# One subtraction per head moved from DVE to GpSimd, with the planned order worked out anew

## The chip, the core and the metric

One core of a Trainium2 chip runs the whole program once. The metric is the device time of that execution in microseconds. The engines are PE (TensorE, matrix products), DVE (VectorE), ACT (ScalarE), POOL (GpSimd) and SP (which here only issues transfers). Each works through its own queue in order and waits at semaphores for the others.

## What is computed

Attention with a causal mask and a bias from running sums, then a mixture layer, then a routed second one:

```python
scores = scale * np.matmul(q, k.transpose(0, 1, 3, 2))
cum = np.cumsum(np.maximum(s, 0.0), axis=-1)
bias = -(cum[:, :, :, None] - cum[:, :, None, :])
scores = np.where(causal, -1000000000.0, scores + np.minimum(bias, 0.0))
attn = softmax(scores); x = np.matmul(attn, v)             # x: 2304 x 512
h = np.maximum(np.maximum(x @ w1, x @ w2), x @ w3)         # 768 wide
x = h @ w_out
e = argmax(x @ w_gate + modality_bias[modality_id])        # 8 experts
out = gate * (np.maximum(x @ w1[e], 0.0) @ w2[e])          # 1024 wide
```

## The kernel before

**Numbers in two parts.** A product is made of fp32 values split in two: the high part is the value rounded to fp32r, the low part is the value minus its high part. A product is then high x high plus high x low plus low x high. Making the parts costs other engines a rounding copy and a subtraction for each operand.

**Attention.** There are 32 heads, in 16 pairs. For a head, `load_x` brings q and k in (`qk_r`, `bufs=3`). `k_high` (L374) copies k's high part into one half of `hl`; `q_high` (L377, ACT) copies q's, in both halves of the partitions; `k_low` (L384) subtracts to make k's low part in the other half of `hl`; `q_low` (L387, POOL) makes q's low part in `q_b`; `k_again` (L380, POOL) makes another copy of k's high part in `k_b`. `k_high` is on POOL for heads 1 to 4 (`CK_POOL`), on ACT for the others. `k_low` is on DVE for all heads. The shape of the last four is 64 x 576.

Then, in five blocks of rows (six pieces, as the longest row is cut in two): `scores` (L394, L395, PE) multiplies `hl` with `hl` and `q_b` with `k_b` into a PSUM bank (three banks); it needs all of the head's parts. `least` (L403, DVE) adds the mask and takes the minimum of the negated scores; `expo` (L410, ACT) makes the exponentials and their sums; `turn` (L415, PE) transposes them, `turned` (L420, DVE or ACT) copies the transposes out of PSUM; `values_of` (L450, PE) multiplies a pair of heads with v; `x_most` and `x_rest` (L456, L460, DVE) multiply by the inverse of the sums, which goes through memory and back (`r_out`, `r_in`) to be spread over the partitions.

**Work beside it.** During attention the first weights of the first mixture layer are converted from a 64-bit form: `wz` on ACT, three steps on DVE (L224, L226, L228), a transfer started by POOL (L231) and a subtraction on POOL (L235). With them PE makes early products of that layer from finished batches, in triples of 128 x 288 (L246, L247, L248; `fill`), 168 triples in all; `fx_high` (ACT) and `fx_low` (L478, POOL) split their inputs, and `filled` (L491) takes the maximum. What is left of the triples follows attention; then come the rest of the first layer and the routed layer.

**What sets the order.** In the attention stage the order of every queue is planned when the program is built. Each piece of work is a `Job` with an engine, an assumed duration in ns, a key, the jobs it follows and the buffers it takes. `planned` plays the queues with these durations: whichever engine can start first gets, among the jobs that can start within 60 ns of the soonest, the one with the lowest key. A key is the head's number times `KEY["T"]` plus an offset for the kind of job; the triples have keys above all others. Jobs marked `lock` on DVE are planned not to overlap with POOL's. The queues then run in this order on the chip, whatever the durations are there. After the stage, the framework's own scheduler orders the instructions.

Of the kernel before, what the change touches and what calls it, by code (L numbers as in the profile page):

```python
# [5 lines left out]
F32 = mybir.dt.float32  # L6
# [3 lines left out]
ALU = mybir.AluOpType  # L10
# [6 lines left out]
T = B * S  # L17
# [63 lines left out]
MIN_NS = {(0, 0): 145, (1, 0): 278, (2, 0): 410, (3, 0): 545, (4, 0): 375, (4, 1): 400}  # L81
SC_NS = {(0, 0): 224, (1, 0): 224, (2, 0): 298, (3, 0): 408, (4, 0): 266, (4, 1): 266}
PT_NS = {"ACT": [420, 420, 275, 485], "DVE": [540, 540, 340, 605]}
CK_POOL = (1, 2, 3, 4)
C_ORDER = [(4, 0), (3, 0), (4, 1), (2, 0), (1, 0), (0, 0)]
T_ORDER = [1, 0, 3, 2]
PT_V = [(1, 0), (3, 0), (0, 1), (2, 1)]
CONV = [(0, 3), (1, 3), (2, 5), (3, 7), (4, 7), (5, 9), (6, 13), (7, 15), (8, 17)]
W_READY, SET_H = 15000, 24
WIRE_FROM, WIRE_TO, WIRE_SLOW = 1300, 900, 1.0  # L90
KEY = {"T": 7489, "wl": 195894, "wz": -70601, "w1": 73283, "wd": 182933, "ws": 159332, "lx": -44441, "lv": -72906, "ck": 7387, "kb": -121032, "kl": 34282, "ql": -113713, "s": 45058, "mn": 54834, "ex": 21338, "ds": 1446, "t": 65914, "dt": 1295, "cp": -47797, "r1": -72927, "r2": -108656, "rt": 37074, "rc": 2313, "rw": -46013, "pv": -70417, "x": 43622, "xc": -76674, "xs": 230686, "fe": -33618}
R_MOE1 = (2, 4, 7)
R_MOE2 = (1, 3, 5)

# [84 lines left out]
def fused_kernel(tc, qk, vd, sd, w64, mod, wg, wgt, mb, we, cst, csi, out):  # L179
    nc = tc.nc  # L180
    V, A, G, P, SP = nc.vector, nc.scalar, nc.gpsimd, nc.tensor, nc.sync
    top = ExitStack()
    with top:
# [73 lines left out]
        with ExitStack() as es:  # L257
# [73 lines left out]
            st, tl = {}, {}  # L331

            def job(name, run, eng, ns, key, **k):
                j = Job(run, eng, ns, key, **k)
                jobs.append(j)
                st[name] = j
                return j

            def at(h, what, n=0):
                return h * KEY["T"] + KEY[what] + n  # L340

# [30 lines left out]
            def k_high(h):  # L372
                hl = tl["hl", h] = qkp.tile([128, 2, S], F32R, name="hl", bufs=HL_BUFS)
                (G.tensor_copy if h in CK_POOL else A.copy)(out=hl[64:128, 0], in_=tl["x", h][64:128, 1])  # L374

            def q_high(h):
                A.copy(out=tl["hl", h][:, 1], in_=tl["x", h][:, 0])  # L377
# [3 lines left out]

            def k_low(h):
                hl = tl["hl", h]
                V.tensor_tensor(out=hl[0:64, 0], in0=tl["x", h][64:128, 1], in1=hl.bitcast(F32)[64:128, 0], op=ALU.subtract)  # L384

            def q_low(h):
                G.tensor_tensor(out=qbs[h % QB_N][0:64], in0=tl["x", h][0:64, 0], in1=tl["hl", h].bitcast(F32)[0:64, 1], op=ALU.subtract)  # L387
# [1 line left out]
            def scores(h, c, k):  # L389
                hl, k_b, q_b = tl["hl", h], tl["k_b", h], qbs[h % QB_N]  # L390
                q0, w = QC[c][0], QC[c][2]
                k0, n = (k * 288, 288) if c == 4 else (0, w)
                s_ps = tl["s_ps", h, c, k] = ps_s.tile([128, 512], F32, name="s_ps")[:, 0:n]
                P.matmul(s_ps, hl[:, 1, q0:q0 + 128], hl[:, 0, k0:k0 + n], start=True, stop=False)  # L394
                P.matmul(s_ps, q_b[:, q0:q0 + 128], k_b[:, k0:k0 + n], start=False, stop=True)  # L395
# [100 lines left out]
            for n, h in CONV:  # L496
                raw, z = Slot("raw"), Slot("z")
                a = job(("wl", n), lambda n=n: w_load(n), "SP", 450, at(h, "wl"), takes=[raw], wire=1500, ready=W_READY)
                for k, (what, eng, ns, u, lock, land) in enumerate([("wz", "ACT", 575, [raw], False, 0), ("w1", "DVE", 346, [], False, 0), ("w1", "DVE", 606, [raw], True, 0), ("w1", "DVE", 610, [raw], True, 0), ("wd", "POOL", 570, [], False, 7000), ("ws", "POOL", 1277, [], False, 0)]):
                    a = job(("w", n), lambda n=n, k=k: w_step(n, k), eng, ns, at(h, what, k), after=[a], takes=[z] if k == 0 else [], uses=u + [z], land=land, lock=lock)  # L500
            rows = job("rows", rows_out, "SP", 1300, -1e8, ready=8700, wire=300)
            turns, highs = None, []
            for h in range(2 * NP):
                p, j = divmod(h, 2)
                s_x, s_k, s_h, s_q, s_e = (Slot(n) for n in ("qk", "kb", "hl", "qb", "e"))
                lx = job(("lx", h), lambda h=h: load_x(h), "SP", 1900 if h == 0 else 1130, at(h, "lx") if h > 2 else -1e9 + h, takes=[s_x], ready=750, wire=1700)
                if j == 0:
                    s_v, s_p, done = Slot("vr"), [], []
                    lv = job(("lv", p), lambda p=p: values_in(p), "SP", 430, at(h, "lv") if p else -9e8, takes=[s_v], wire=1300, ready=2000)
                ck = job(("ck", h), lambda h=h: k_high(h), "POOL" if h in CK_POOL else "ACT", 671 if h in CK_POOL else 575, at(h, "ck"), after=[lx], takes=[s_h], uses=[s_x], ready=0 if h else 6640)  # L510
                cq = job(("cq", h), lambda h=h: q_high(h), "ACT", 580, at(h, "ck", 1), after=[lx, ck], uses=[s_x, s_h])
                if h > 1:
                    lk = job(("lk", h), lambda h=h: load_k(h), "SP", 300 if h > 1 else 450, at(h, "lx", 1) if h > 1 else -2e8 + h, after=[rows], takes=[s_k], wire=100, ready=7800)
                kb = job(("kb", h), lambda h=h: k_again(h), "POOL", 657, at(h, "kb"), after=[lx, lk] if h > 1 else [lx], takes=[s_k] if h < 2 else [], uses=[s_x, s_k])
                if h < 2:
                    lk = job(("lk", h), lambda h=h: load_k(h), "SP", 300 if h > 1 else 450, at(h, "lx", 1) if h > 1 else -2e8 + h, after=[kb], uses=[s_k], wire=100, ready=7800)
                kl = job(("kl", h), lambda h=h: k_low(h), "DVE", 780, at(h, "kl"), after=[ck], uses=[s_x, s_h], lock=True, tail=10)
                ql = job(("ql", h), lambda h=h: q_low(h), "POOL", 1410, at(h, "ql"), after=[cq], takes=[s_q], uses=[s_x, s_h])
                ex = {}
                for n, (c, k) in enumerate(C_ORDER):  # L520
                    bank = Slot("s")
                    a = job(("s", h, c, k), lambda h=h, c=c, k=k: scores(h, c, k), "PE", SC_NS[c, k], at(h, "s", n * KEY["ds"]), after=[kl, cq, kb, ql, lk], takes=[bank], uses=[s_h, s_q, s_k])
                    a = job(("mn", h, c, k), lambda h=h, c=c, k=k: least(h, c, k), "DVE", MIN_NS[c, k], at(h, "mn", n * KEY["ds"]), after=[a] + ([st["mn", h, *C_ORDER[0]]] if n else []), takes=[s_e] if n == 0 else [], uses=[bank, s_e], lag=145 * k)
                    if k or c < 4:
                        ex[c] = job(("ex", h, c), lambda h=h, c=c: expo(h, c), "ACT", EXP_NS[c], at(h, "ex", n * KEY["ds"]), after=[a], uses=[s_e], tail=0)
                done += ex.values()
                for n, i in enumerate(T_ORDER):
                    bank, s_t = Slot("t"), Slot("pt")
                    turns = job(("t", h, i), lambda h=h, i=i: turn(h, i), "PE", 109 * len(BANKS[i][0]) - 82, at(h, "t", n * KEY["dt"]), after=[ex[c] for c in sorted({c for c, _ in BANKS[i][0]})] + [turns] * (turns is not None), takes=[bank], uses=[s_e], tail=247)
                    eng = "DVE" if (i, j) in PT_V else "ACT"  # L530
                    s_p.append((s_t, job(("cp", h, i), lambda h=h, i=i: turned(h, i), eng, PT_NS[eng][i], at(h, "cp", n * KEY["dt"]), after=[turns], takes=[s_t], uses=[bank])))
                if j:
                    bank, s_r, s_0, s_o = Slot("t"), Slot("rb"), Slot("t"), Slot("o")
                    a = job(("r1", p), lambda p=p: sums(p), "ACT", 180, at(h, "r1"), after=done, lag=125)
                    a = job(("r2", p), lambda p=p: inverse(p), "DVE", 130, at(h, "r2"), after=[a])
# [303 lines left out]
        for w in range(NW):  # L839
# [25 lines left out]
            for i in range(MW // 128):  # L865
                t = w * (MW // 128) + i
# [181 lines left out]
```

## Time and profile before

| | us |
|---|---|
| Median of three runs | 749.87 (748.5 to 750.04) |
| The profiled execution | 748.16 |
| Its span, first to last instruction | 746.4 |
| PE busy | 713.3 (96%) |
| DVE busy | 523.9 (70%) |
| ACT busy | 403.1 (54%) |
| POOL busy | 184.7 (25%) |

The profile is of one execution. Its rows give the busy time of an engine, the durations of instructions, and for each idle time the event that ended it ("<-" and the engine and line that released it). The shares over the whole span mix stages with different limits, so the rows below are taken by stretch. A duration of an instruction on DVE or POOL includes time in which it was started but stood still. Durations of neighbouring instructions of an engine overlap a little, so busy time is less than their sum.

### The profile page before, as it was taken

The numbers are of one execution on the slowest core, as the hardware profiler recorded it, in microseconds if no ns is written. First come the engines' busy times: TensorE is split into PE (matmuls) and PEld (weight loads), VectorE is DVE, ScalarE is ACT, GpSimd is POOL, SyncE is SP. The second block draws the span as 40 slices with busy tenths as digits, with TensorE's granted clock in tenths as the row PEclk, the third lists the DMA queues.
The fourth block names the chain that finished last, engine by engine and source line by source line (L and its number), as shares of the span: only waits on it lengthen the run. The fifth ranks groups of instructions, "written<-read, shape, count | busy, mean of one in ns | idle before, by whom it ended". The sixth has DMA issues, their size and how long they took to land. (4 is left out here: it accounts for less than half of the span.)

```text
span 746.4 us, 13653 instructions
## 1 busy us (share of the span) xinstructions
PE 713.3 (96%) x4602; PEld 638.7 (86%) x4602; DVE 523.9 (70%) x1567; ACT 403.1 (54%) x988; POOL 184.7 (25%) x206
## 2 busy tenths in 40 slices
PE   4889999999999999999999999999999999999996
PEld 3677878779888989999999998999899988999884
DVE  5899999998856972494676786675776556575540
ACT  5888898799753541222222222446556565565631
POOL 6555556454201220001010101033132222221101
PEclk9999999999999999999999999999999999999999
DMA  7565775756116530100101011568487565666610
GB/s 212 150 194 151 213 204 161 212 151 167 48 62 212 164 113 0 40 15 12 54 12 64 22 49 36 197 178 249 125 256 262 203 241 188 237 213 220 220 41 19
DMA packets 43536, 103.84 MB, mean 139 GB/s; under 512 B 9472, under 2 KB 13472, under 8 KB 43456
## 3 DMA queue, kind: packets, MB, share of 16 engines
q1 hardware_dynamic: 35808, 86.04, 37.2%
q0 software_dynamic: 4912, 11.82, 5.2%
q10 hardware_dynamic: 2736, 5.01, 1.8%
q8 instruction: 38, 0.62, 0.3%
q14 instruction: 42, 0.34, 0.1%
HBM read 88.83 MB, written 12.18 MB: 135 GB/s over the span
## 5 line engine op out<-in xcount | busy, mean ns | idle before, releaser
L246 PE MATMUL a_ps<-xh,w_h 128*128 128x384 f32 (+2 forms) x492 | 161.2, 328 | 3.0 <-ACT h L489 1.7
L247 PE MATMUL a_ps<-xl,w_h 128*128 128x384 f32 (+2 forms) x492 | 157.6, 320 | 0.3 <-POOL xl L478 0.3
L248 PE MATMUL a_ps<-xh,w_l 128*128 128x384 f32 (+2 forms) x492 | 156.8, 320 | 0.0
L750 DVE TENSOR_TENSOR e_l<-e_raw,e_h 128x512 fp32r<-128x512 f32 x160 | 103.3, 684 | 12.6 <-ACT e_h L749 11.2
L749 ACT CAST e_h<-e_raw 128x512 fp32r<-128x512 f32 x160 | 92.8, 622 | 14.9 <-DMA e_raw<-in_we 6.1
L246 PEld LDWEIGHTS a_ps<-xh,w_h 128*128 128x128 f32 x492 | 92.9, 189 | 4.8 <-ACT h L489 2.2
L410 ACT ACTIVATE e<-e,mn 128x448 f32<-128x448 f32 (+4 forms) x160 | 88.7, 556 | 11.5 <-DVE mn L403 11.3
L247 PEld LDWEIGHTS a_ps<-xl,w_h 128*128 128x128 f32 x492 | 92.9, 189 | 1.5 <-POOL xl L478 0.9
L248 PEld LDWEIGHTS a_ps<-xh,w_l 128*128 128x128 f32 x492 | 92.5, 188 | 0.1
L780 PE MATMUL h_ps<-x2t,e_h 128*128 128x256 f32 x288 | 81.0, 282 | 0.0
L781 PE MATMUL h_ps<-x2t,e_l 128*128 128x256 f32 x288 | 80.9, 282 | 0.0
L779 PE MATMUL h_ps<-x2t,e_h 128*128 128x256 f32 x288 | 80.5, 282 | 0.0
L394 PE MATMUL s_ps<-hl 128*128 128x288 f32 (+1 forms) x192 | 66.7, 357 | 13.8 <-ACT augk L267 7.5
L658 POOL DMA_INDIRECT table<-meta,si x18 | 19.1, 1063 | 241.0 <-DVE nm L646 83.8
L633 DVE CUSTOM_DVE_ANT_0 junk<-x,wg 128x512 bf16<-128x512 f32 x96 | 65.8, 685 | 17.2 <-ACT x L711 16.3
L415 PE MATMUL t_ps<-ident,e 128*128 128x128 f32 x480 | 72.0, 283 | 3.9 <-DVE pt L420 3.3
L403 DVE CUSTOM_DVE_ANT_0 e<-s_ps,mask 128x288 f32<-128x288 f32 (+4 forms) x160 | 63.2, 424 | 6.5 <-PE s_ps L395 5.8
L415 PEld LDWEIGHTS t_ps<-ident,e 128*128 128x128 f32 x480 | 58.5, 145 | 7.0 <-DVE pt L420 4.3
L387 POOL TENSOR_TENSOR q_b<-qk_r,hl 64x576 fp32r<-64x576 f32 x32 | 48.7, 1523 | 57.9 <-ACT hl L377 51.5
L395 PE MATMUL s_ps<-k_b,q_b 66*128 66x288 f32 (+1 forms) x192 | 59.5, 319 | 3.0 <-POOL q_b L387 3.0
L809 PE MATMUL y_ps<-e_h,gh 128*128 128x512 f32 x152 | 61.5, 405 | 0.4 <-ACT gh L801 0.4
L811 PE MATMUL y_ps<-e_h,gl 128*128 128x512 f32 x152 | 60.7, 399 | 0.0
(178 smaller groups left out, 1484.1 us busy)
## 6 DMA issues: line engine op xcount, KB each, us to landing
e_raw<-in_we SPq DMA_DIRECT2D x80, 512.0 KB
w_raw<-in_w SPq DMA_DIRECT2D x24, 512.0 KB
qk_r<-in_qk SPq DMA_DIRECT2D x31, 288.0 KB
v_r<-in_vd SPq DMA_DIRECT2D x16, 320.0 KB
rb<-r_d SPq DMA_DIRECT2D x32, 160.0 KB
qk_r<-in_qk SPq DMA_DIRECT2D x32, 144.0 KB
x2d<-x ACTq DMA_DIRECT2D x18, 256.0 KB
w_h<-w_z POOLq DMA_DIRECT2D x9, 256.0 KB, 5.9
```

Of the source, the lines that this page charges most:

```text
L246: P.matmul(a_ps, wh[:, c], xh, start=c == 0, stop=False)
L247: P.matmul(a_ps, wh[:, c], xl, start=False, stop=False)
L248: P.matmul(a_ps, wl[:, c], xh, start=False, stop=c == 3)
L394: P.matmul(s_ps, hl[:, 1, q0:q0 + 128], hl[:, 0, k0:k0 + n], start=True, stop=False)
L410: A.activation(out=ec, in_=ec, func=ACTF.Exp, bias=tl["mn", h][:, c:c + 1], scale=-1.0, accum_out=tl["l", p][:, j, c:c + 1])
L415: P.transpose(out=t_ps[:, n * 128:(n + 1) * 128], in_=e_bufs[h % E_N][:, EOFF[c] + kb * 128:EOFF[c] + (kb + 1) * 128], identity=ident)
L633: V.tensor_tensor_reduce(out=junk, in0=x2, in1=wg_sb[ei // 2][:, ei % 2, :], scale=1.0, scalar=0.0, op0=ALU.mult, op1=ALU.add, accum_out=l ...
L749: A.copy(out=h, in_=raw[:, a])
L750: V.tensor_tensor(out=lo, in0=raw[:, a], in1=h.bitcast(F32), op=ALU.subtract)
L779: P.matmul(h_ps, w(hs, f, c), xt[:, 0, c], start=c == 0, stop=False)
L780: P.matmul(h_ps, w(hs, f, c), xt[:, 1, c], start=False, stop=False)
L781: P.matmul(h_ps, w(ls, f, c), xt[:, 0, c], start=False, stop=c == 3)
```

## The change

`k_low` moves from DVE to POOL for heads 1 to 31; head 0 keeps it on DVE. `k_high` of heads 1 to 4 moves from POOL to ACT. The planner's table of keys is another one, and some assumed durations are other ones: the weight steps on DVE, the roundings on ACT and the scores are planned as longer, the weight steps no longer as locked against POOL.

```diff
-CK_POOL = (1, 2, 3, 4)
+CK_POOL = ()
+KL_DVE = (0,)
...
-KEY = {"T": 7489, "wl": 195894, "wz": -70601, "w1": 73283, "wd": 182933, "ws": 159332, "lx": -44441, "lv": -72906, "ck": 7387, "kb": -121032, "kl": 34282, "ql": -113713, "s": 45058, "mn": 54834, "ex": 21338, "ds": 1446, "t": 65914, "dt": 1295, "cp": -47797, "r1": -72927, "r2": -108656, "rt": 37074, "rc": 2313, "rw": -46013, "pv": -70417, "x": 43622, "xc": -76674, "xs": 230686, "fe": -33618}
+KEY = {"T": 13121, "wl": 335509, "wz": 23759, "w1": 144307, "wd": 156003, "ws": 321816, "lx": 164276, "lv": -213741, "ck": 5481, "kb": 19101, "kl": -60043, "ql": -58751, "s": 264284, "mn": 24364, "ex": 43536, "ds": 50, "t": 176453, "dt": 3418, "cp": 54562, "r1": 16757, "r2": -10485, "rt": 112017, "rc": 23647, "rw": -7037, "pv": -19979, "x": -161664, "xc": 53429, "xs": 81013, "fe": 51163}
...
-                V.tensor_tensor(out=hl[0:64, 0], in0=tl["x", h][64:128, 1], in1=hl.bitcast(F32)[64:128, 0], op=ALU.subtract)
+                (V if h in KL_DVE else G).tensor_tensor(out=hl[0:64, 0], in0=tl["x", h][64:128, 1], in1=hl.bitcast(F32)[64:128, 0], op=ALU.subtract)
...
-                kl = job(("kl", h), lambda h=h: k_low(h), "DVE", 780, at(h, "kl"), after=[ck], uses=[s_x, s_h], lock=True, tail=10)
+                kl = job(("kl", h), lambda h=h: k_low(h), "DVE" if h in KL_DVE else "POOL", 850 if h in KL_DVE else 1415, at(h, "kl"), after=[ck], uses=[s_x, s_h], lock=h in KL_DVE, tail=10 if h in KL_DVE else 0)
```

In the new kernel every line number below the first of these is one higher: L385 is `k_low`, L388 `q_low`, L381 `k_again`.

**POOL's queue at the start of attention**, from the copies of k for heads 0 and 1 on (`hl<-qk_r` at L374 is `k_high`, `q_b` is `q_low`). Before:

```order
L380 CAST k_b<-qk_r 64x576 x2
L374 CAST hl<-qk_r 64x576
L387 ISA
L387 TENSOR_TENSOR q_b_129<-qk_r,hl 64x576
L387 TENSOR_TENSOR q_b_130<-qk_r,hl 64x576
```

Now:

```order
L381 CAST k_b<-qk_r 64x576 x2
L388 ISA
L388 TENSOR_TENSOR q_b_129<-qk_r,hl 64x576
L385 TENSOR_TENSOR hl<-qk_r,hl 64x576
L388 TENSOR_TENSOR q_b_130<-qk_r,hl 64x576
```

`k_high` of head 1 has left the place ahead of the first `q_low`, and `k_low` of head 1 stands between the first two.

**POOL's queue in the middle of the stage**, where weights are converted beside the heads (`w_l` and `w_h` are weight steps, `xl` is `fx_low`). Before:

```order
L387 TENSOR_TENSOR q_b_129<-qk_r,hl 64x576
L380 CAST k_b<-qk_r 64x576
L235 TENSOR_TENSOR w_l<-w_z,w_h 128x512
L478 TENSOR_TENSOR xl<-x_521,xh 128x288
L387 TENSOR_TENSOR q_b_130<-qk_r,hl 64x576
L380 CAST k_b<-qk_r 64x576
L231 DMA w_h<-w_z 128x512
L387 TENSOR_TENSOR q_b_131<-qk_r,hl 64x576
```

Now:

```order
L385 TENSOR_TENSOR hl<-qk_r,hl 64x576
L388 TENSOR_TENSOR q_b_130<-qk_r,hl 64x576
L479 TENSOR_TENSOR xl<-x_515,xh 128x288
L232 DMA w_h<-w_z 128x512
L385 TENSOR_TENSOR hl<-qk_r,hl 64x576
L388 TENSOR_TENSOR q_b_131<-qk_r,hl 64x576
L381 CAST k_b<-qk_r 64x576
```

Each head has one more subtraction there, directly ahead of its `q_low`.

**DVE's queue behind the second pair's normalisation** (`x_521` and `x_515` are the output of attention, `e_135` the exponentials' buffer of one head, `pt` a transpose copied out). Before:

```order
L403 ISA e_135,mn<-s_ps,mask 128x448
L403 ISA mn 128x1
L384 TENSOR_TENSOR hl<-qk_r,hl 64x576
L420 COPY pt<-t_ps 128x512
L403 ISA e_135,mn<-s_ps,mask,mn 128x288
```

Now:

```order
L457 TENSOR_TENSOR x_515<-o_ps,rb 128x512
L461 TENSOR_TENSOR x_515<-t_ps,rb 128x64
L404 ISA e_135,mn<-s_ps,mask 128x448
L404 ISA mn 128x1
L404 ISA e_135,mn<-s_ps,mask,mn 128x288
```

The subtraction that stood between two minimums and ahead of a copy is gone.

On PE, counted over the whole queue, 83 of the 168 triples stood ahead of the last product with v and 85 behind it; now 61 stand ahead of it and 107 behind.

## Rows read from the trace of the kernel before

Each group says its view. In timelines a row is the start and the duration in us, then the engine, the line and the operation; the brackets hold the idle time before it and what ended it.

**Rows 1.** Busy us by stretch: PE, PEld, DVE, ACT, POOL; clock, DMA share, GB/s.

```profile
0.00:20.00 20.00, 9.22 (x35) 8.26 (x36) 11.78 (x33) 10.39 (x23) 13.08 (x39) 1.00 0.78 218
20.00:60.00 40.00, 34.53 (x245) 27.92 (x245) 35.97 (x116) 35.28 (x103) 21.88 (x22) 0.96 0.56 162
60.00:120.00 60.00, 56.24 (x434) 47.40 (x432) 57.04 (x167) 52.12 (x149) 33.80 (x35) 1.00 0.67 191
120.00:180.00 60.00, 57.01 (x430) 46.82 (x429) 54.34 (x163) 53.10 (x149) 29.98 (x28) 0.97 0.62 174
227.00:300.00 73.00, 69.69 (x445) 67.51 (x445) 47.36 (x84) 25.83 (x51) 8.76 (x9) 1.00 0.37 125
20.00:227.00 207.00, 194.71 (x1481) 162.40 (x1481) 182.39 (x564) 174.56 (x499) 95.75 (x93) 0.98 0.53 152
```

**Rows 2.** Whom PE waited for, 20 to 227 us: total, times, longest.

```profile
PE s_ps L394 <- DVE mn L403: 5.3, 8, 1.5
PE t_ps L415 <- DVE pt L420: 3.3, 3, 2.1
PE t_ps L431 <- DVE x L460: 1.3, 1, 1.3
PE t_ps L431 <- DVE mn L403: 0.7, 1, 0.7
PE s_ps L394 <- DVE hl L384: 0.7, 1, 0.7
```

**Rows 3.** DVE, line 384, 20 to 227 us: group; then min/median/max ns.

```profile
L384 DVE TENSOR_TENSOR hl<-qk_r,hl 64x576 fp32r<-64x576 f32 x29 | 29.2, 1009 | 1.8 <-ACT hl L374 1.0
L384 DVE TENSOR_TENSOR hl<-qk_r,hl x29: 751/754/2599, 23.2 to 199.2; 64x576 fp32r<-64x576 f32 x29
```

**Rows 4.** Timeline of DVE, POOL and PE at 48 to 53 us: start, duration.

```profile
48.97 0.62 DVE L403 CUSTOM_DVE_ANT_0 e<-s_ps,mask 128x448 f32<-128x448 f32 x1
49.63 2.60 DVE L384 TENSOR_TENSOR hl<-qk_r,hl 64x576 fp32r<-64x576 f32 x1
...
48.19 1.43 POOL L387 TENSOR_TENSOR q_b<-qk_r,hl 64x576 fp32r<-64x576 f32 x1 [0.19 <-ACT hl L377]
49.59 0.79 POOL L478 TENSOR_TENSOR xl<-x,xh 128x288 fp32r<-128x288 f32 x1
50.35 1.26 POOL L235 TENSOR_TENSOR w_l<-w_z,w_h 128x512 fp32r<-128x512 f32 x1
...
52.89 1.09 PE L415 MATMUL t_ps<-ident,e 128*128 128x128 f32 x8 [2.13 <-DVE pt L420]
```

**Rows 5.** POOL, line 387: min/median/max ns; its wait for ACT, 20-227 us.

```profile
L387 POOL TENSOR_TENSOR q_b<-qk_r,hl x32: 1395/1430/1949, 9.1 to 199.6; 64x576 fp32r<-64x576 f32 x32
...
POOL q_b L387 <- ACT hl L377: 50.1, 21, 4.6
```

**Rows 6.** Timeline of POOL and PE at the start.

```profile
7.91 1.08 POOL L374 CAST hl<-qk_r 64x576 fp32r<-64x576 f32 x1
9.08 3.33 POOL L387 TENSOR_TENSOR q_b<-qk_r,hl 64x576 fp32r<-64x576 f32 x2
...
11.08 0.61 PE L395 MATMUL s_ps<-k_b,q_b 66*128 66x288 f32 x1 [3.04 <-POOL q_b L387]
```

**Rows 7.** Line 246, 227 to 300 us; two triples in the stage.

```profile
L246 PE MATMUL a_ps<-xh,w_h x149: 288/302/407, 226.8 to 299.9; 128*128 128x288 f32 x85, 128*128 128x384 f32 x64
...
89.12 0.30 PE L246 MATMUL a_ps<-xh,w_h 128*128 128x288 f32 x1
89.52 0.30 PE L246 MATMUL a_ps<-xh,w_h 128*128 128x288 f32 x1
```

**Rows 8.** DVE, line 226, 0 to 250 us: min/median/max; the group.

```profile
L226 DVE SCALAR_TENSOR_TENSOR w_z<-w_raw,w_z x17: 674/691/1815, 29.0 to 248.1; 128x512 int32<-128x512 int32 x17
...
L226 DVE SCALAR_TENSOR_TENSOR w_z<-w_raw,w_z 128x512 int32<-128x512 int32 x17 | 14.4, 851 | 0.2
```

**Rows 9.** Busy time from 160 to 180 us, columns as in rows 1.

```profile
160.00:180.00 20.00, 19.63 (x158) 16.09 (x157) 16.51 (x58) 18.90 (x54) 10.58 (x11) 1.00 0.60 170
```

More of the change, by code (lines that the diff above doesn't have):

```diff
@@ L498, in fused_kernel @@
                 a = job(("wl", n), lambda n=n: w_load(n), "SP", 450, at(h, "wl"), takes=[raw], wire=1500, ready=W_READY)
-                for k, (what, eng, ns, u, lock, land) in enumerate([("wz", "ACT", 575, [raw], False, 0), ("w1", "DVE", 346, [], False, 0), ("w1", "DVE", 606, [raw], True, 0), ("w1", "DVE", 610, [raw], True, 0), ("wd", "POOL", 570, [], False, 7000), ("ws", "POOL", 1277, [], False, 0)]):
+                for k, (what, eng, ns, u, lock, land) in enumerate([("wz", "ACT", 575, [raw], False, 0), ("w1", "DVE", 600, [], False, 0), ("w1", "DVE", 1000, [raw], False, 0), ("w1", "DVE", 1000, [raw], False, 0), ("wd", "POOL", 570, [], False, 7000), ("ws", "POOL", 1277, [], False, 0)]):
                     a = job(("w", n), lambda n=n, k=k: w_step(n, k), eng, ns, at(h, what, k), after=[a], takes=[z] if k == 0 else [], uses=u + [z], land=land, lock=lock)
@@ L509, in fused_kernel @@
                     lv = job(("lv", p), lambda p=p: values_in(p), "SP", 430, at(h, "lv") if p else -9e8, takes=[s_v], wire=1300, ready=2000)
-                ck = job(("ck", h), lambda h=h: k_high(h), "POOL" if h in CK_POOL else "ACT", 671 if h in CK_POOL else 575, at(h, "ck"), after=[lx], takes=[s_h], uses=[s_x], ready=0 if h else 6640)
-                cq = job(("cq", h), lambda h=h: q_high(h), "ACT", 580, at(h, "ck", 1), after=[lx, ck], uses=[s_x, s_h])
+                ck = job(("ck", h), lambda h=h: k_high(h), "POOL" if h in CK_POOL else "ACT", 671 if h in CK_POOL else 640, at(h, "ck"), after=[lx], takes=[s_h], uses=[s_x], ready=0 if h else 6640)
+                cq = job(("cq", h), lambda h=h: q_high(h), "ACT", 600, at(h, "ck", 1), after=[lx, ck], uses=[s_x, s_h])
                 if h > 1:
@@ L521, in fused_kernel @@
                     bank = Slot("s")
-                    a = job(("s", h, c, k), lambda h=h, c=c, k=k: scores(h, c, k), "PE", SC_NS[c, k], at(h, "s", n * KEY["ds"]), after=[kl, cq, kb, ql, lk], takes=[bank], uses=[s_h, s_q, s_k])
+                    a = job(("s", h, c, k), lambda h=h, c=c, k=k: scores(h, c, k), "PE", SC_NS[c, k] + 40, at(h, "s", n * KEY["ds"]), after=[kl, cq, kb, ql, lk], takes=[bank], uses=[s_h, s_q, s_k], tail=210)
                     a = job(("mn", h, c, k), lambda h=h, c=c, k=k: least(h, c, k), "DVE", MIN_NS[c, k], at(h, "mn", n * KEY["ds"]), after=[a] + ([st["mn", h, *C_ORDER[0]]] if n else []), takes=[s_e] if n == 0 else [], uses=[bank, s_e], lag=145 * k)
```

## The prediction, made before the changed kernel was run

> **What bounds the kernel now.** I read first the busy time of the engines in stretches [rows 1]. The attention stage ends with the last product with v, at about 227 us; PE then does the left-over early MoE products and the MoE proper with hardly a gap, and the work after 300 us is not touched by the change. So the time is PE's total work, which both kernels share, plus what PE loses. From 20 to 227 us PE is busy 194.71 of 207 us: it loses 12.3 us there. In the same stretch DVE is busy 182.39 us (88.1%), ACT 174.56 (84.3%) and POOL 95.75 (46%). In 60 to 120 us DVE stands at 57.04 of 60.
>
> Then, whom PE waited for in that stretch [rows 2]: the five kinds of wait that sum to over 0.5 us make 5.3 + 3.3 + 1.3 + 0.7 + 0.7 = 11.3 of the 12.3 us, every one of them on DVE. The scores' banks come free when DVE has taken their minimum, the transposes' banks when DVE has copied them. DVE is the limit of this stage, and it is one because it is late in its queue, not because one operation is long.
>
> A second loss follows the first: the granted clock is 0.96 over 20 to 60 us and 0.97 over 120 to 180 us [rows 1], so some of the time there ran at the lower of the two levels, 1.2 instead of 2.4 GHz. Lost work: 0.04 x 40 + 0.03 x 60 = 3.4 us. Together 15.7 us can be had in this stage, and no more.
>
> What the low part of k costs DVE: 29 instructions in the stretch, 29.2 us, mean 1009 ns, though the median is 754 and the shortest 751 [rows 3]. The difference is standing still: the one at 49.63 us took 2.60 us, and the transposes behind it on PE waited 2.13 us for the copy that stood behind it on DVE [rows 4].
>
> The reason stands in the same rows: POOL ran two subtractions from 49.59 to 51.61 us, and `k_low` ended 0.6 us after them [rows 4].
>
> **The change, part by part.**
>
> *k_low off DVE.* 31 of 32 go. In the stretch DVE loses 29.2 us of 182.4 and stands at 153.2.
>
> *k_low on POOL.* The same shape with two SBUF inputs is q_low there: 1430 ns in the median of 32 [rows 5]. 29 x 1.43 = 41.5 us; POOL goes from 95.75 to 137.2. Now two operations for a head stand in one queue, 2.86 us, where k_low on DVE ran beside q_low on POOL. A head's first score waits for both. What hides this is that POOL can run ahead: today q_low waits 50.1 us in the stretch for ACT's rounded q [rows 5], so POOL is idle for more than its new load. If the cover is gone, see the slower rival. Today PE waits for POOL only at the very start; I bound new waits by 0 and by one such wait as that of the start, 3.0 us [rows 6], and take a third, +1.0.
>
> *The four k_high that POOL made go to ACT.* They are those of heads 1 to 4, at the start. POOL does k_high of head 1 from 7.91 to 8.99 and only then q_low of head 0, at 9.08, for which PE's second matmul waits until 11.08 [rows 6]. Without it q_low can start at 7.9: 1.2 us at most, 0 if the first minimums on DVE set the pace of the following scores. I take -1.0. k_low of head 1 then stands between q_low 0 and q_low 1 on POOL; 7.9 + 3 x 1.43 = 12.2, which is when q_low 1 ends today (9.08 + 3.33 = 12.41). ACT gets four copies, each at most the 1.08 us of the one on POOL; over the first 20 us it is busy 10.39 [rows 1], so they find room: nothing. Without that room, 4.3 us.
>
> *The new order.* It has 61 of the 168 triples of early MoE products before the last product with v, where the old one has 83 (85 of them follow it, as the trace also shows [rows 7]). A triple takes 0.40 us at full clock (89.12 to 89.52 [rows 7]); 22 of them are 8.9 us. These move from inside the stage to the stretch behind it. That is no gain and no loss of its own, but it sets the scale: the stage must end 8.9 us sooner, at 218, for the kernel to break even.
>
> *DVE's weight steps.* They still meet POOL. The one of L226 has a mean of 851 against a median of 691 [rows 8], 0.16 us of standing still; 27 steps in the stage make 4.3 us, and with POOL busy half again as often some 2 us more, between 0 and 4. DVE has 20% to spare, so I take +0.5 on PE's path.
>
> *How much of the 15.7 us goes.* Suppose the stage shortens by 8.9 + 6 = 15 us, to 192 us. Then ACT's 174.6 are 91%, DVE's 153.2 + 2 are 81%, POOL's 137.2 are 71%, PE is at 97%. The trace has a stretch with that mix: 160 to 180 us, with ACT at 18.90 of 20, DVE at 16.51 and PE idle for only 0.37 [rows 9]. By that row the idle time over 192 us would be 3.6 us, a gain of 8.7. Against it: ACT then has to hold 91% over the whole stage in a fixed order, where DVE, the limit today, held 88%. Holding no more than 88% it gives 198 us and no gain. So the idle time saved is between 0 and 8.7, with 15.7 as the end for everything, clock included. I take 5.0, somewhat beyond the middle, since every wait that is seen is one on DVE; the clock loss follows in proportion, 5.0/12.3 x 3.4 = 1.4, say 1.5.
>
> Behind the stage PE is idle for 73 - 69.69 = 3.3 us in 227 to 300 [rows 1], while DVE and ACT convert weights. They start this sooner and PE has more triples to cover it: 0 to -2, I take 0.
>
> **The sum**: -1.0 (start) - 5.0 (idle) - 1.5 (clock) + 1.0 (POOL) + 0.5 (weight steps) = -6.0 us. The profiled execution took 748.16 us (span 746.4 and 1.8 us around it), 1.7 below the median of the three runs, 749.87. Set against its own time the sum gives 742.2; against the median, 743.9. I predict the median.
>
> **Rivals.**
>
> *ACT takes DVE's place* (748 to 751). DVE's relief shortens the stage by what the moved triples take, 8.9 us, and no more, since ACT at 88% sets the pace; PE's waits are then put down to ACT's exponentials and copies. For it: ACT is the next busiest and the change gives it work. Against it: in 160 to 180 us it went to 94%. With the start's -1.0: 749.
>
> *POOL becomes the pacer* (slower). Between 60 and 180 us POOL is busy 33.80 + 29.98 = 63.8 us [rows 1]. By time, 120/207 of the 41.5 us of new work fall there, 24, which makes 88. If POOL's waits for ACT's rounded q stay, by time 29 of the 50.1 us [rows 5], because k_low and q_low of a head are both asked for at the same late point, that is 117 of 120, and with the waits on transfers this part gets no shorter. The stage then ends where it ends today, but with 22 triples fewer done: 8.9 - 1.0 (start) = 8 us later, 758. It decides from the point where the stage ends less than 8.9 us sooner because of POOL: in these 120 us POOL may wait 120 - 5 - 88 = 27 us (5 being their share of the 8.9). For it: the queue is in order, so a wait of q_low or of a weight step blocks the next head's k_low. Against it: POOL's waits today come from heads that start late because DVE is late; and k_low, whose input ACT makes before q_low's, stands ahead of q_low in the new order and can use part of them.
>
> *A shared port keeps DVE waiting* (a rival on the rows alone). If DVE's other instructions stood still for POOL as k_low does, 1009 - 754 = 255 ns in the mean, the 192 minimums (six for each of 32 heads) would wait half as long again with POOL half as busy again: 192 x 0.13 = 25 us more of DVE. That takes the 29.2 us of relief nearly whole; DVE is the limit again at 178 us and the kernel ends as before, 750. The row against it: while POOL ran q_low from 48.19 to 49.62 us, DVE's 448-wide minimum from 48.97 took 0.62 us [rows 4], in a stretch in which k_low took 2.60. So I give it little.
>
> The Trainium skill speaks on both sides here. Its page Perfetto Trace Analysis (Optimizing Scalar/DVE Operations) says that moving work between DVE and GpSimd might not help, as they share an SBUF port: by that the sum would be 750. Its page SBUF — State Buffer (Who interferes with whom) narrows it to DVE instructions in a two-port mode or with two SBUF inputs: the minimums read one input from PSUM, and by that the sum stays. The rows agree with the second, 0.62 us against 2.60.
>
> *All waits on DVE vanish*: -15.7 - 1.2 + 1 = -16, 734.
>
> **How the numbers follow.** The forecast (738 to 748) gets 0.60, all waits gone 0.09, ACT as the limit 0.15, the port 0.03, POOL as the pacer 0.13. The range 735 to 752 leaves out half of the best case and nearly all of the POOL case. A measurement of this kernel tells 0.2%, 1.5 us, from no change. Faster: 0.59 + 0.09 + 0.05 of the ACT case, 0.73. Same: 0.12. Slower: 0.15, POOL and the rest. The forecast's end at 748 is where "faster" begins.
>
> **What would show it.** Right: 31 k_low on POOL near 1.43 us; DVE near 80% in the stage; the last product with v ending near 212 us (today the triples behind it start at 226.8 [rows 7]); PE's idle time from 20 us to there near 7, with fewer waits on minimums and copies; q_low of head 0 at 7.9. Wrong: PE waits on POOL's k_low or q_low of over 3 us, or on ACT of over 6; a last product with v after 218 us. If the idle time is gone but the clock's row stays below 0.97, only the second term has failed.

## The result, and the profile after

The changed kernel took 740.31 us in the median of four runs (737.85 to 742.0), the kernel before 749.95 beside it (748.5 to 750.09). The ratio is 0.9873, with a 95% interval from 0.9841 to 0.9906: 9.5 us less (7 to 12), where -6.0 was forecast. The profiled execution took 739.44 us, its span is 737.3, against 748.16 and 746.4 before. In the changed kernel lines behind the constants are one higher (`k_low` L385, `q_low` L388).

Busy time over the whole span (first row of the page), then by stretch with the columns of [rows 1]. The stage now ends at 209.2 us, so its row is 20 to 209.2.

```profile
PE 709.3 (96%) x4602; PEld 634.5 (86%) x4602; DVE 498.3 (68%) x1536; ACT 403.9 (55%) x992; POOL 225.5 (31%) x233
```

```profile
0.00:20.00 20.00, 9.01 (x34) 8.41 (x35) 11.69 (x31) 14.14 (x30) 16.20 (x39) 1.00 0.69 198
20.00:60.00 40.00, 36.34 (x266) 28.30 (x264) 35.27 (x118) 36.58 (x107) 31.76 (x30) 1.00 0.62 182
60.00:120.00 60.00, 59.55 (x470) 49.80 (x469) 52.37 (x181) 57.58 (x168) 49.25 (x45) 1.00 0.72 212
120.00:180.00 60.00, 57.45 (x449) 47.30 (x448) 49.80 (x176) 56.69 (x164) 45.49 (x40) 1.00 0.57 168
20.00:209.20 189.20, 182.42 (x1415) 149.35 (x1413) 155.87 (x533) 169.74 (x491) 130.17 (x117) 1.00 0.58 168
209.20:300.00 90.80, 87.14 (x558) 84.48 (x557) 52.38 (x97) 30.81 (x66) 11.04 (x12) 1.00 0.31 104
```

PE's busy time falls from 713.3 to 709.3 us, 4.0 less, and its idle time from 746.4 - 713.3 = 33.1 to 28.0, 5.1 less. That is the 9.1 us of span. Where they lie is read from the rows. Idle from 20 us to the last product with v: 189.20 - 182.42 = 6.8, against 12.3 [rows 1] (which runs 0.2 us past the end). First 20 us: 10.99 against 10.78. Behind the stage, to 300 us: 90.80 - 87.14 = 3.7 against 3.3. So the idle time was saved inside the stage. The granted clock is 1.00 in every row, where two rows stood at 0.96 and 0.97 before: the 3.4 us of work that the lower clock had cost there came back. Over the whole execution it is less: behind 700 us the clock is 0.95 for 37.3 us, against 0.98 for 46.4 before, and the mean went from 0.994 to 0.997, which is 4.5 us lost before and 2.2 now. So some 2.3 of the 4.0 us of busy time are the clock; where the rest comes from is not shown.

The end of the stage, on PE (start, duration):

```profile
206.32 2.81 PE L451 MATMUL o_ps<-pt,v_r 128*64 128x512 f32 x20
208.96 0.29 PE L451 MATMUL t_ps<-pt,v_r 128*64 128x64 f32 x4
```

It ends at 209.2 instead of 226.8, 17.6 us sooner, of which 8.9 are the triples that moved behind it. Whom PE waited for, 20 to 227 us, as in [rows 2]:

```profile
PE o_ps L451 <- ACT pt L421: 1.8, 2, 1.6
PE t_ps L416 <- DVE x L461: 1.8, 2, 1.4
PE t_ps L432 <- DVE r L428: 1.1, 1, 1.1
PE s_ps L395 <- DVE mn L404: 0.5, 2, 0.3
PE a_ps L247 <- DVE h L492: 0.4, 1, 0.4
PE t_ps L416 <- DVE pt L421: 0.3, 2, 0.2
```

Five kinds of wait on DVE made 11.3 us before. The largest, 5.3 on the scores' banks, is 0.5; the next, 3.3 on copies, is 0.3; the wait on `k_low` is gone. What is left is 5.9 us in many places, 1.8 of it on ACT, none on POOL.

`k_low` (count, then min/median/max ns), and what POOL waits for at it:

```profile
L385 POOL TENSOR_TENSOR hl<-qk_r,hl x31: 1402/1422/1801, 8.9 to 177.6; 64x576 fp32r<-64x576 f32 x31
...
L385 DVE TENSOR_TENSOR hl<-qk_r,hl x1: 1108/1108/1108, 6.4 to 6.4; 64x576 fp32r<-64x576 f32 x1
```

```profile
POOL hl L385 <- ACT hl L375: 21.6, 12, 3.9
```

1.422 us in the median on POOL, nearly twice the 754 ns on DVE [rows 3]. POOL's wait of 50.1 us for the rounded q [rows 5] is gone from the list; its largest wait for a head is now one of 21.6 us for the rounded k. Most of the new work went into time in which POOL had waited.

### The profile page after: what moved, and what is told of

It is laid out like the page before. It is cut to its first block, busy times and chain, and to the rows that moved or that the text cites. A ratio compares the mean times of both kernels' runs of the same rounds, so it can differ in the third digit from the quotient of the medians.

```text
span 737.3 us, 13677 instructions
## 1 busy us (share of the span) xinstructions
PE 709.3 (96%) x4602; PEld 634.5 (86%) x4602; DVE 498.3 (68%) x1536; ACT 403.9 (55%) x992; POOL 225.5 (31%) x233
## 5 line engine op out<-in xcount | busy, mean ns | idle before, releaser
L395 PE MATMUL s_ps<-hl 128*128 128x288 f32 (+1 forms) x192 | 64.4, 345 | 8.3 <-DVE hl L385 7.7
L416 PEld LDWEIGHTS t_ps<-ident,e 128*128 128x128 f32 x480 | 55.8, 142 | 7.4 <-DVE x L461 2.9
L396 PE MATMUL s_ps<-k_b,q_b 66*128 66x288 f32 (+1 forms) x192 | 57.4, 316 | 3.3 <-DMA k_b<-augk 3.3
L811 PE MATMUL y_ps<-e_l,gh 128*128 128x512 f32 x152 | 60.0, 395 | 0.0
```

The lines of the kernel that those rows point to most:

```text
L416: P.transpose(out=t_ps[:, n * 128:(n + 1) * 128], in_=e_bufs[h % E_N][:, EOFF[c] + kb * 128:EOFF[c] + (kb + 1) * 128], identity=ident)
```

## The experiments

Each ratio is to runs of the kernel before on the same chip; a thousandth is 0.75 us. It is not the quotient of two medians and can differ from that by up to 0.003. The changed kernel's 0.9873 is the mark for those that start from it.

**Theory:** DVE was late in its queue, and taking a sixth of its load in the stage away (29.2 of 182.4 us) is the gain. **Rivals:** the gain is the new order's; or it is the standing still of `k_low` for POOL, not DVE's load; and, for what comes next, ACT or POOL as the new limit.

### The move alone and the order alone

The kernel before with its plan unchanged, the subtraction issued on POOL in the place that the plan had for DVE:

```diff
-                V.tensor_tensor(out=hl[0:64, 0], ...
+                (G if h else V).tensor_tensor(out=hl[0:64, 0], ...
```

> The kernel before, its planned order unchanged, but the low part of k for heads 1 to 31 is issued on POOL at the place in the sequence that was planned for DVE. Theory (DVE's load is the cost, any order can use the relief): DVE loses 29 us in the stage, PE's waits on DVE shrink from 11 to some 5 us, 742 to 747 us. Rival (the new order is what helps; the move alone puts k_low badly into POOL's queue): 749 us or more, with PE waiting for POOL. The number of triples ahead of the last product with v stays at 83, so the stage would end near 220 us by the theory, near 227 by the rival.

Measured: 740.53 us, 0.9847 (0.9808 to 0.9886). PE's last product with v, and the stage by stretch:

```profile
220.57 0.29 PE L450 MATMUL t_ps<-pt,v_r 128*64 128x64 f32 x4
```

```profile
20.00:220.80 200.80, 192.22 (x1480) 160.94 (x1478) 154.56 (x534) 173.52 (x499) 134.67 (x121) 0.98 0.57 159
```

The stage ends 11.6 us later than with the new order, with 22 triples (8.9 us) more in it, and the kernel is as fast. PE is idle for 8.6 us there. The old order, made for another placement, is enough for the whole gain, and no worth of the moved triples by themselves can be seen.

The other way round, the new order with `k_low` on DVE for all heads:

```diff
-                (V if h in KL_DVE else G).tensor_tensor(out=hl[0:64, 0], ...
+                V.tensor_tensor(out=hl[0:64, 0], ...
```

> The changed kernel, its planned order unchanged, but the low part of k is issued on DVE for all heads. Theory (load on DVE): DVE has 182 us again in a stage that the order wants to end at 209, 96%; the stage ends later, 750 to 756 us, and PE's waits are put down to DVE again. Rival (the order is what helps): 740 to 743 us, as the changed kernel.

Measured: 762.76 us, 1.0154 (1.0122 to 1.0186). Whom PE waited for, and `k_low` on DVE:

```profile
PE s_ps L395 <- DVE mn L404: 9.1, 12, 2.9
PE t_ps L432 <- DVE r L428: 4.4, 4, 2.2
```

```profile
L385 DVE TENSOR_TENSOR hl<-qk_r,hl x32: 753/914/3510, 6.2 to 203.7; 64x576 fp32r<-64x576 f32 x32
```

The waits on minimums are back, larger than before, and single subtractions took up to 3.51 us, 2.8 of it standing still. The longest, and the next wait of PE:

```profile
129.01 3.51 DVE L385 TENSOR_TENSOR hl<-qk_r,hl 64x576 fp32r<-64x576 f32 x1
```

```profile
133.20 0.59 PE L395 MATMUL s_ps<-hl 128*128 128x320 f32 x1 [2.93 <-DVE mn L404]
```

POOL ran two subtractions in that time, between 128.67 and 131.89 us; the new order, made for `k_low` on POOL, does not keep the two apart. Behind this wait the granted clock was 0.50 from 134 to 136 us. So the move is worth 1.0154 - 0.9873 = 0.028, 21 us, in the new order and 0.0153, 11.5 us, in the old one. With `k_low` on DVE the new order is a loss, with it on POOL no gain that can be told.

Half of the move, in the old order, odd heads alone:

```diff
-                V.tensor_tensor(out=hl[0:64, 0], ...
+                (G if h % 2 else V).tensor_tensor(out=hl[0:64, 0], ...
```

> The kernel before, in its own order, with k_low on POOL for the odd heads alone, half of the change's load moved (about -15 us from DVE, +22 us on POOL). Half of the copies that can stand still for POOL are left on DVE. If the gain goes with DVE's load and POOL has room (my forecast's mechanism): half of what the whole move gave in this order (740.5 against 750.0), 745. If the last of the move is neutral because POOL is then at its edge (0.6 us per us added, as the doubled runs had it): the first half gives nearly all, 739 to 742. If POOL in two-operation heads holds each head up whatever the rest does: 748 to 751.

Measured: 745.24 us, 0.9927 (0.9904 to 0.995). `k_low` on both engines, and PE's two largest waits:

```profile
L384 DVE TENSOR_TENSOR hl<-qk_r,hl x16: 753/755/2595, 6.5 to 184.8; 64x576 fp32r<-64x576 f32 x16
L384 POOL TENSOR_TENSOR hl<-qk_r,hl x16: 1401/1417/1771, 8.3 to 193.3; 64x576 fp32r<-64x576 f32 x16
```

```profile
PE s_ps L394 <- DVE mn L403: 3.1, 6, 0.8
PE t_ps L415 <- DVE pt L420: 2.8, 2, 2.1
```

Half the move gives half the gain, within the intervals: 0.0073 of 0.0153. The waits lie between those of before (5.3 and 3.3) and those of the whole move in this order (2.9 and 0.9). There is no sign of an edge on POOL up to the whole move.

The kernel before, with its keys and its other assumed durations, but with a planner that knows that `k_low` runs on POOL, and so makes another order:

```diff
+KL_DVE = (0,)
...
-                V.tensor_tensor(out=hl[0:64, 0], ...
+                (V if h in KL_DVE else G).tensor_tensor(out=hl[0:64, 0], ...
...
-                kl = job(("kl", h), lambda h=h: k_low(h), "DVE", 780, ...
+                kl = job(("kl", h), lambda h=h: k_low(h), "DVE" if h in KL_DVE else "POOL", 850 if h in KL_DVE else 1415, ...
```

> The kernel before with the low part of k on POOL for heads 1 to 31, and the planner told so (1415 ns on POOL, not locked); keys, other durations and k_high as before. It puts 62 triples ahead of the last product with v, as the changed kernel does with 61. Theory (the relief of DVE is the gain, the order is secondary): 738 to 744 us. Rival (the new keys and durations were needed for the gain): 746 us or more.

Measured: 744.62 us, 0.9899 (0.9862 to 0.9936). That lies between the 744 and the 746 of the two expectations. It is not better than the old order left alone; whether worse, the intervals do not say (by the medians 744.62 against 740.53).

### Load, or standing still?

A reduction of the mask's 128 x 576 elements behind each `k_low`, on DVE, its result unused:

```diff
+                if h:
+                    V.tensor_reduce(out=idle_v, in_=mask, axis=AX.X, op=ALU.max)
```

> The changed kernel with a reduction on DVE behind each low part of k of heads 1 to 31 (one 128x576 input of SBUF, the result unused): some 0.65 us each, 20 us more on DVE, of a kind that reads one input. If DVE's load is what costs: DVE back to some 173 of 189 us, 92%, 744 to 748 us. Rival (what cost was k_low standing still for POOL, and the copies behind it): the filler does not stand still, 740 to 742 us.

Measured: 748.57 us, 0.9968 (0.9947 to 0.999).

```profile
L388 DVE TENSOR_REDUCE idle_v<-mask x31: 690/745/753, 7.1 to 188.5; 128x1 f32<-128x576 f32 x31
```

31 x 745 ns are 23 us of load. 29 of them lie in the stage, 21.4 us, 0.73 of the 29.2 us that the change took away, and the longest is hardly longer than the median: these never stood still. They give back 0.9968 - 0.9873 = 0.0095, 7.1 us of 9.5: 0.75 of the gain, by the intervals some 0.4 to 1. (DVE's busy time over the whole span rises to 514.5 us: 16.2 of the 25.6 that the change took away, 0.63.) So load on DVE costs by itself, also where nothing stands still.

That it is all is not shown. The run of the same order with `k_low` on DVE has 35.5 us of it in the stage (29 of 1223 ns in the mean) and costs 21 us, though it takes 41 us off POOL: 0.59 us for each, where the filler costs 0.33 (7.1 for 21.4). Much of the difference is the clock: the four executions of that run have a mean granted clock of 0.9865, which is 10.3 us lost, the changed kernel 0.997, 2.2 us. Less these 8 us it is 13 for 35.5, 0.37, near the filler's (an estimate). Where standing still makes a long wait, as at 133.20, it costs clock besides its time; what `k_low`'s place ahead of a head's scores adds, no run tells apart.

### What the other engines bear

`k_low` made twice on POOL, for all heads but the first (+44 us), and for odd heads alone (+22 us); and the rounding of q made twice on ACT (+18.6 us):

```diff
+                if h:
+                    G.tensor_tensor(out=hl[0:64, 0], in0=tl["x", h][64:128, 1], in1=hl.bitcast(F32)[64:128, 0], op=ALU.subtract)
```

```diff
+                if h % 2:
+                    G.tensor_tensor(out=hl[0:64, 0], in0=tl["x", h][64:128, 1], in1=hl.bitcast(F32)[64:128, 0], op=ALU.subtract)
```

```diff
+                A.copy(out=tl["hl", h][:, 1], in_=tl["x", h][:, 0])
```

> The changed kernel with each low part of k on POOL subtracted twice (the same values are written again): 31 x 1.42 = 44 us more on POOL in the stage, DVE as in the changed kernel. If POOL has the slack that its 70 to 75% share suggests and can run ahead: 740 to 745 us. Rival (POOL is already nearly the pacer, its queue in order): its 137 + 44 = 181 us of a stage of 189 make 96%, PE waits for POOL, 750 us or more.

> The changed kernel with the low part of k subtracted twice on POOL for the odd heads alone: 22 us more on POOL, half of the doubling for all heads, which cost 24 us. If each us on POOL costs alike (POOL is on the path all along): 752 us. If POOL has slack that the full doubling used up: 741 to 746 us.

> The changed kernel with each q_high on ACT copied twice (the same values are written again): 32 x 0.58 = 18.6 us more on ACT. In the changed kernel ACT is busy 57.6 of 60 us between 60 and 120 us. If ACT is what limits the stage now: 750 us or more. If ACT still has room (its waits elsewhere absorb the copies): 743 us or less; in between, both.

Measured: 764.68 us, 1.0182 (1.0146 to 1.0217); 753.99 us, 1.0044 (1.0019 to 1.0068); 749.0 us, 0.998 (0.9956 to 1.0003). The middle of the stage and one wait of PE with POOL's load added for all heads, then the same with ACT's:

```profile
60.00:120.00 60.00, 55.01 (x417) 44.74 (x417) 49.00 (x156) 50.27 (x143) 56.16 (x47) 0.97 0.57 173
120.00:180.00 60.00, 52.24 (x390) 41.91 (x390) 48.17 (x156) 50.50 (x146) 55.86 (x47) 1.00 0.61 177
```

```profile
PE s_ps L398 <- POOL q_b L390: 7.9, 9, 1.5
```

```profile
60.00:120.00 60.00, 56.32 (x430) 46.04 (x430) 49.69 (x171) 59.24 (x165) 44.96 (x40) 1.00 0.65 195
120.00:180.00 60.00, 55.95 (x432) 45.45 (x429) 48.18 (x164) 58.83 (x163) 43.05 (x39) 1.00 0.61 181
```

```profile
PE o_ps L452 <- ACT pt L422: 4.6, 6, 2.1
PE t_ps L417 <- ACT pt L422: 3.2, 8, 0.8
```

POOL reaches 94% and ACT 99%. From the mark, by the ratios: 23.2 us for 44 on POOL (0.53 us of kernel time per us of load), 12.8 for 22 (0.58), 8.0 for 18.6 on ACT (0.43), 7.1 for 23 on DVE (0.31; the expectations that follow still have 0.6 and 0.36, from the medians). The first two came out as the costlier of the expectations had it, the third between its two. No engine takes such work without a price, POOL with the least busy time the least of all. A reason could be that its queue is in order and that q_low and k_low stand ahead of all scores of a head, but this is not shown: the doubled operations on POOL and ACT lie on that path, the filler on DVE does not, so the prices compare places as well as engines. With odd heads alone doubled PE's waits on POOL from 20 to 240 us come to 2.5 us, and the kernel is 12.8 us slower. It stays open, too, why the 41 us that the move itself put on POOL show no such price and the next 22 do.

### Taking load off POOL

If POOL's load costs that much, less of it could gain. The weights' subtraction moved to DVE, and the second copy of k's high part moved to DVE:

```diff
-            (G if early else V).tensor_tensor(out=lo, in0=z, ...
+            V.tensor_tensor(out=lo, in0=z, ...
```

```diff
-                G.tensor_copy(out=k_tile(h)[0:64], ...
+                (V if h > 1 else G).tensor_copy(out=k_tile(h)[0:64], ...
```

> The changed kernel, with the subtraction that makes the weights' low part (w_l, L236) on DVE instead of POOL, in the same order. It takes about 12.7 us off POOL (10 of 1.27 us) and gives DVE some 6 to 9 us. Theory (after the doubled runs: POOL's load is now on the path, about 0.6 us of kernel time for each us of it, DVE's about 0.36): -7.6 + 2.2 to 3.2 = -5 us against the changed kernel, about 735, PE waits on DVE a little up. Rival (POOL is at a bound only where work is added, and taking work away frees nothing, as ACT's 96% is the limit): no gain, and DVE's new work costs 2 to 3 us, 742 to 744. Second rival (a subtraction with two SBUF inputs on DVE stands still for POOL, as k_low did before): mean of the ten steps over 1.5 us, 742 or more.

> The changed kernel, with the second copy of k's high part (k_b, L381) of heads 2 to 31 on DVE instead of POOL, in the same order: about 20 us off POOL (30 of 0.66 us). Theory (POOL on the path at about 0.6 us per us, DVE at 0.36): -12 on POOL; on DVE 30 copies of 0.35 to 0.75 us, 11 to 22 us, +4 to +8: 732 to 737 in all. Rival (the copies from SBUF to SBUF stand still for POOL or make POOL stand still): DVE's copies over 1 us in the mean or POOL's subtractions over 1.6, and 742 or more. Rival (POOL's relief is worth nothing, ACT being the limit): 744 to 748.

Measured: 740.72 us, 0.9884 (0.9825 to 0.9944); 747.08 us, 0.9962 (0.9934 to 0.999). The copies on DVE:

```profile
L381 DVE CAST k_b<-qk_r x30: 452/456/1719, 16.4 to 184.0; 64x576 fp32r<-64x576 f32 x30
```

The theory of a price per us that holds both ways has fallen: 735 and 732 to 737 were expected. In the second the 29 copies in the stage take 21.7 us of DVE (mean 755 ns, median 456: many stood still, the longest took 1.72 us). At 0.31 that is 6.7 us, and the kernel is 0.0089, 6.7 us, slower: if a copy costs what the filler did, the 21.8 us taken off POOL (busy 225.5 to 203.7) gave back nothing that can be seen, within some 3 us. POOL's subtractions became no longer (1467 and 1446 ns in the mean, 1447 and 1432 in the changed kernel). That is what the last of its rivals expected, 744 to 748, but not that ACT is the reason. In the first, DVE has 11 such steps in the stage, 9.6 us, where the changed kernel has 2, 1.3 us; the 8.3 more would be 2.6, and 0.8 was measured, within its interval of 4.5 us either way. More load on POOL costs; a gain from less was not seen. What would have to be relieved next is open.

### The start

`k_high` of heads 1 to 4 back on POOL, in the new order:

```diff
-                (G.tensor_copy if h in CK_POOL else A.copy)(out=hl[64:128, 0], ...
+                (G.tensor_copy if h in (1, 2, 3, 4) else A.copy)(out=hl[64:128, 0], ...
```

> The changed kernel in its order, but k_high of heads 1 to 4 is issued on POOL again. My prediction's start term (their leaving POOL brings the first scores 1.0 us forward) expects 741 to 742 us, 1 us more than the changed kernel, and the first second matmul about 1 us later than its 11.57. What the changed kernel's trace suggests instead (the first scores wait for the bias rows, whose subtraction on DVE stood still for POOL, 1.85 instead of 0.97 us) expects no difference, 740 us.

Measured: 738.68 us, 0.984 (0.98 to 0.9879). POOL, DVE and PE at the start in the changed kernel (start, duration; in brackets the wait):

```profile
7.02 1.78 POOL L388 TENSOR_TENSOR q_b<-qk_r,hl 64x576 fp32r<-64x576 f32 x1
...
7.57 1.85 DVE L269 TENSOR_TENSOR augk<-s,augk 32x576 fp32r<-32x576 f32 x1
...
8.88 1.80 POOL L385 TENSOR_TENSOR hl<-qk_r,hl 64x576 fp32r<-64x576 f32 x1
...
11.57 0.58 PE L396 MATMUL s_ps<-k_b,q_b 66*128 66x288 f32 x1 [3.31 <-DMA k_b<-augk]
```

the same DVE step in the kernel before, where its line is L268:

```profile
7.48 0.97 DVE L268 TENSOR_TENSOR augk<-s,augk 32x576 fp32r<-32x576 f32 x1 [0.17 <-ACT augk L267]
```

and DVE's L269 and PE's second product with `k_high` back on POOL:

```profile
7.18 1.10 DVE L269 TENSOR_TENSOR augk<-s,augk 32x576 fp32r<-32x576 f32 x1
```

```profile
10.72 0.58 PE L396 MATMUL s_ps<-k_b,q_b 66*128 66x288 f32 x1 [2.84 <-DMA k_b<-augk]
```

With the copies on ACT, POOL starts `q_low` at 7.02, and the subtraction on DVE that makes the bias rows (`augk`, two SBUF inputs) meets it: 1.85 us, against 0.97 before and 1.10 here. The bias rows go to `k_b` by a transfer, and PE waits for that until 11.57, against 11.08 [rows 6] and 10.72 here. So this part of the change costs the start 0.5 to 0.9 us; over the whole kernel the gain from taking it back is 0.0033, 2.5 us, too little to be told, though both expectations had 740 or more.

Both things together, `k_high` back and the weights' subtraction on DVE:

> The changed kernel with k_high of heads 1 to 4 back on POOL (738.7 by itself, -1.6) and the weights' low part w_l on DVE (740.7 by itself, +0.4). If the start's gain is real and the weights' step is worth nothing: 738 to 740. If POOL's relief pays where the start loads POOL more: 734 to 737. If w_l on DVE costs by DVE's load (0.36 of 9.6 us): 742.

Measured: 740.9 us, 0.9863 (0.9811 to 0.9916): nothing beyond the changed kernel. The fastest here, 0.984, 0.9847, 0.9863, 0.9873 and 0.9884, cannot be told apart.

## Why the prediction was right, and where it was not

**The bound was right.** DVE was the limit by being late. The move alone and half of it agree with that in sign and size, and load put back on DVE costs again.

**Idle time, -5.0: right.** 12.3 to 6.8 is -5.5. DVE stands at 155.87 of 189.2 us (82%; 80 forecast), the stage ends at 209.2 (212). The rows gave 0 to 8.7 and the 5.0 was chosen between them, so that it came so near is in part luck. The 6.8 us hold all of PE's waits in the stage, those put down as POOL's and the weight steps' too, for which +1.5 stood in the sum: net -3.5 was forecast.

**Clock, -1.5: the term that was mis-sized most.** In the stage of the two profiled executions all 3.4 us came back, and 2.3 over their whole spans. "The clock loss follows in proportion" does not fit the rows. Stretches of 2 us before, columns of [rows 1], where the first loss lay:

```profile
32.00:34.00 2.00, 1.38 (x11) 1.15 (x10) 1.91 (x11) 1.98 (x8) 1.00 (x2) 1.00 0.86 247
34.00:36.00 2.00, 0.82 (x6) 0.55 (x4) 0.85 (x3) 1.46 (x5) 1.05 (x1) 1.00 0.85 236
36.00:38.00 2.00, 1.19 (x8) 0.97 (x9) 1.94 (x7) 1.57 (x4) 1.27 (x3) 1.00 0.09 33
38.00:40.00 2.00, 2.00 (x13) 2.00 (x12) 1.81 (x10) 1.58 (x8) 0.54 (x1) 0.58 0.41 95
40.00:42.00 2.00, 2.00 (x11) 1.98 (x12) 1.28 (x7) 0.96 (x5) 0.00 (x0) 0.57 0.52 180
```

PE was idle for 0.62, 1.18 and 0.81 us in three neighbouring rows, and then worked at 0.58 and 0.57: partly at 1.2 GHz. The other loss is at 144 to 148 us, behind three rows with 1.4 us of idle time:

```profile
144.00:146.00 2.00, 1.71 (x8) 1.70 (x9) 1.94 (x7) 1.38 (x5) 0.00 (x0) 0.53 0.91 256
146.00:148.00 2.00, 2.00 (x12) 2.00 (x11) 1.46 (x6) 1.42 (x3) 0.29 (x1) 0.61 0.84 256
```

The whole 3.4 us lay in these two places, not with the idle time as such. The first stretch in the changed kernel:

```profile
28.00:30.00 2.00, 1.45 (x10) 1.07 (x8) 2.00 (x11) 1.95 (x8) 0.04 (x1) 1.00 0.74 235
30.00:32.00 2.00, 0.88 (x4) 0.34 (x6) 2.00 (x3) 2.00 (x5) 1.93 (x2) 1.00 0.18 60
32.00:34.00 2.00, 2.00 (x23) 1.15 (x19) 2.00 (x2) 1.98 (x9) 1.94 (x2) 1.00 0.00 0
34.00:36.00 2.00, 1.32 (x10) 0.93 (x8) 2.00 (x4) 1.26 (x3) 1.14 (x3) 1.00 0.70 188
36.00:38.00 2.00, 1.58 (x13) 1.53 (x14) 2.00 (x9) 1.71 (x6) 1.93 (x3) 1.00 0.98 310
```

As much idle time, 0.55 + 1.12 + 0.68 + 0.42 = 2.8 us, but with a full row in its middle, and the clock stayed at 1.00. So what a clock row is worth has to be looked up place by place: does the change touch the waits ahead of that fall?

One execution is not enough for that. With the move alone in the old order the first place stayed (0.91 over 20 to 60 us) in the profiled execution; that is the slowest of four, 742.62 us with a mean clock of 0.993, and the fastest took 736.87 us at 1.000. The 58 executions of the kernel before that stand beside the experiments have mean clocks of 0.987 to 0.998, 0.9926 on average, which is 5.6 us lost; the four of the changed kernel have 0.996 to 0.998, 2.2 us. By these the clock's part of the gain is 3.3 us, more than twice the forecast.

**Start, -1.0: wrong in sign**, +0.2 by the idle time of the first 20 us, +0.5 by the second product. `q_low` of head 0 did start early (7.02; 7.9 was forecast), but the next to be late were the bias rows, made worse by that very early start. I had named the first minimums as the next bound, and not looked at what else the second product reads.

**POOL's waits, +1.0: none.** The cover held: POOL's 50.1 us of waits took up the new load. But "POOL is idle for more than its new load" is no sufficient reason; the doubled runs paid as much per us for 22 us as for 44, though POOL had been at 82% at most between 60 and 180 us.

**Weight steps, +0.5:** the three steps take 33.4 us for 36 in the stage, against 29.5 for 35 (the forecast had counted 27); +3.9 us on DVE, the upper end of what was bounded. No wait of PE can be put down to it.

**The new order, neutral: right**, by the move in the old order. **Behind the stage, 0:** +0.4.

With the measured terms: -5.5 - 4.0 (busy time, the clock in it) + 0.2 + 0.4 = -8.9; the span gives -9.1. Against the forecast's -6.0 that is 2.5 more for the busy time, 2.0 more for the idle time (net), 1.2 less at the start and 0.4 less behind the stage: errors of both signs, which in part cancel.

**The rivals.** *ACT takes DVE's place:* fell. It held 57.58 of 60 us, 96%, from 60 to 120 us with PE at 99%; the 88% was not its limit. With its load raised by 18.6 us, the kernel is 8.0 us slower and PE waits for it. *POOL the pacer:* not at this load. *The port:* fell in the form in which it was priced, on the minimums. The largest minimum has the same mean on both sides, with POOL 39% busier from 20 to 227 us (133.08 against 95.75). Groups of DVE, before and after:

```profile
L403 DVE CUSTOM_DVE_ANT_0 e<-s_ps,mask 128x448 f32<-128x448 f32 x30 | 18.6, 619 | 0.6 <-PE s_ps L395 0.5
```

```profile
L404 DVE CUSTOM_DVE_ANT_0 e<-s_ps,mask 128x448 f32<-128x448 f32 x30 | 18.6, 619 | 0.0
```

The Trainium skill, SBUF — State Buffer (Who interferes with whom), says that DVE contends with GpSimd's reads where it has two SBUF inputs, or in a two-port mode, which copies can enter, and not else. The traces agree in all four cases: the minimums, with one input from PSUM, 619 and 619 ns; the mask's reduction, with one input, 690 to 753; `augk`, with two, 1.85 for 0.97 us; the copies 0.456 in the median and 1.72 at most. Its page Perfetto Trace Analysis (Optimizing Scalar/DVE Operations), by which such a move might not help, is not borne out here, where it did help: 1.3% less time, though the subtraction takes 1.42 us instead of 0.75.

## What to carry to other kernels

Where the waits of the bounding engine are all on one engine that is late in its queue, move work off it, even to an engine that takes twice as long for it, if that one is waiting for inputs at that point anyway. Idle time of the other engine is no proof that it can bear more: try half of the move and more than the move. Price the idle time by the stretch that resembles the new mix, but each loss of clock by the waits ahead of its own place, and read the clock from several executions. When a wait at the start is removed, look at all that the waiting instruction reads, and at whether the earlier start collides with what makes it.

## What was not expected of the hardware

- Load added to DVE, ACT or POOL in this stage cost 0.3 to 0.6 us per us in the places tried, with POOL's, at 82% busy or less between 60 and 180 us, the dearest; load taken off POOL gave nothing that was seen.
- In the profiled execution of the kernel before all of the clock's loss in the stage lay at two places, 38 to 42 and 144 to 148 us, and the wait of 2.13 us that ended at 52.9 us [rows 4], the longest of the stage, was followed by none (1.00 to 58 us).
- The mean clock of one kernel differs between executions, 0.987 to 0.998 in 58 of the kernel before.
- A subtraction on DVE stood still for POOL for up to 2.8 us (3.51 against 0.75), where the order does not keep the two apart.
